# Attention plus two MLP blocks on one core: where the scores of the last 64 queries are computed, and in which PSUM tile

## Chip, cores and metric

One Trainium2 chip, one of its cores. The time is the device time of one execution in microseconds (us): 447.11 us is the median of three executions of the kernel before (447.08 to 447.6). Engines are called by the names of the profile: PE is the matrix engine (PEld its weight loads), DVE the vector engine, ACT the scalar engine, POOL the GpSimd engine, SP the engine that issues the DMAs.

## What is computed

```python
def _attn_ref(q, k, v):                      # 2 batches, 12 heads, 448 tokens, 64 columns per head
    scores = scale * np.matmul(q, k.transpose(0, 1, 3, 2))
    scores = np.where(mask, -1000000000.0, scores)          # causal: keys behind the query
    scores = scores - np.max(scores, axis=-1, keepdims=True)
    attn = np.exp(scores)
    attn = attn / (np.sum(attn, axis=-1, keepdims=True) + 1e-09)
    return np.matmul(attn, v).astype(np.float32)
...
x = attn_out, heads side by side             # 896 tokens x 768
x = silu(x @ w_in) @ w_out                   # 768 -> 2048 -> 768
x = solu_layernorm(x @ w_in2) @ w_out2       # 768 -> 1024 -> 768
```

All data are fp32. The change lies in the attention alone, at the scores.

## The kernel before, in words

**Stages.** The attention takes about the first 80 us; then come the four matrix products (fp32 split into a high and a low part, three products each), which keep PE filled to the end.

**The attention loop.** The loop of line 342 has one iteration per head pair (two heads j = 0, 1 of one batch), 12 pairs in all, plus four iterations in which only late steps are left. Each engine works through its instructions in the order in which the program writes them, so the order of the statements in the loop is a schedule written out by hand. An iteration i does for pair i the scores, their maxima and exponentials; for pair i - 1 the reciprocals of the sums and the normalisation (`recip`, `norm`); for pair i - 2 the transposes of the normalised weights (`transp`) and their copies out of PSUM (`evict`); for pair i - 3 the product with v (`pv`); for pair i - 4 the split of that product's result into a high part (`pv_hi`, line 192, ACT) and a low part (`pv_lo`, line 197, DVE).

**Scores.** The queries of a head are cut into three blocks of 128 (c = 0, 1, 2) and a rest of 64 (c = 3). Because of the causal mask block c needs 128 (c + 1) key columns: 128, 256, 384, and 448 for the rest. For c = 0, 1, 2 there is a matrix product for each of the two heads, on one half of PE's rows each (line 117). For c = 3 both heads' 64 queries stand side by side in one zero-padded stationary operand of 128 rows (`q3s`), so that one product serves both heads; its 448 columns are cut into two halves of 224, one in each bank (line 109). Each fp32 product runs on PE as two passes, so the profile counts twice as many matmuls as the code writes.

**PSUM tiles of the scores.** The pool `pss` has two tiles of two banks each, `sa` and `sb`, one buffer each (bank j is head j). Before, `sa` holds the 384-column scores and, behind them in the same banks, the 128-column scores; `sb` holds the 256-column scores and behind them the two 224-column halves. A tile is written anew for the next pair only when all its readers are done. The readers are the maxima (`maxes`, line 128): one DVE instruction per block and head adds the mask, writes the result to SBUF and keeps the row's extremum. Their order on DVE is that of `UNITS`: the two 384-column blocks, the reciprocals of the pair before (lines 138, 139), `pv_lo`, the two 128-column blocks, the two 256-column blocks, the 448-column block, then the copies `evict` of groups 2 and 3 (line 173), one normalisation (line 146), and, from iteration 8 on, a piece of weight conversion (`feed`, lines 217 to 225) ahead of the next pair's maxima. In iteration 1 the order differs: four normalisations of pair 0 stand on DVE behind the maxima of pair 1.

**PSUM tiles of the transposes.** The pool `psx` has four one-bank buffers that go round. An iteration takes six: the transposes' groups 0 to 4 and the tile of `pv`. So group 3 gets the buffer in which the `pv` of the iteration before stands, and must wait until `pv_lo` has read it; group 4 gets the buffer of group 0, which ACT copies out in the same iteration. Groups 0 to 3 hold 3, 3, 4 and 2 transposes, group 4 holds 4.

PE's order in an iteration is thus: scores c = 2, 0, 1, 3; transposes groups 0, 1, 2, 3, 4; `pv`. After the last live iteration the space of `pss` goes to the first matrix product (`g1drain`, line 298).

Of the kernel before, what the change touches and what calls it, by code (L numbers as in the profile page):

```python
# [8 lines left out]
F32 = mybir.dt.float32  # L9
# [6 lines left out]
B, H, S, D = 2, 12, 448, 64  # L16
# [26 lines left out]
def fused(ctx, tc, qT, kT, vv, vt, w1, w2, w3, w4, gl, out):  # L43
    nc = tc.nc
    PS = bass.MemoryType.PSUM

    def pool(name, bufs=1, **kw):
        return tc.alloc_tile_pool(name=name, bufs=bufs, **kw)
# [12 lines left out]
    with tc.manual_schedule():  # L61
        att = pool("att", 2)
        psx = pool("psx", 4, space=PS)
        pss = pool("pss", 1, space=PS, side="right")
# [3 lines left out]
        QB, EB = 4, 3  # L68
        q3s = [att.tile([128, 2, C], F32, name=f"qt{n}", tag=f"qt{n}", bufs=1) for n in range(QB)]
# [28 lines left out]
        st, scs = {}, {}  # L98

        def scores(p, c):  # L100
            k, q, _ = raws[p]
            if c == 2:
                scs[p, "a"] = pss.tile([128, 2, 512], F32, name="sa", tag="sa")
            elif c == 1:
                scs[p, "b"] = pss.tile([128, 2, 512], F32, name="sb", tag="sb")
            elif c == 3:
                t = scs[p, 0, 3] = scs[p, "b"][:, :, 256:256 + S // 2]
                for j in range(2):
                    nc.tensor.matmul(t[:, j], q3s[p % QB], k[:, S // 2 * j:S // 2 * (j + 1)],
                                     start=True, stop=True)  # L110
                return
            t = scs[p, "b" if c == 1 else "a"]
            lo = 384 if c == 0 else 0
            for j in range(2):
                dst = scs[p, j, c] = t[:, j, lo:lo + wide(c)]
                r = slice(64 * j, 64 * j + 64)
                nc.tensor.matmul(dst, q[r, 128 * c:128 * c + 128], k[r, :wide(c)], start=True, stop=True)

        def ep(p, u):
            return es[p % EB][:, AT[u]:AT[u] + 4].rearrange("q b k -> q (b k)")[:, :wide(u[1])]  # L120

        def maxes(p, u):
            if p not in st:
                st[p] = att.tile([128, 4, 7], F32, name="st", tag="st", bufs=4)
            o, m = ep(p, u), (mask3 if u[1] == 3 else mask)[:, S - wide(u[1]):]
            if u[1] == 3:
                o, m = (a.rearrange("q (z k) -> q z k", z=2) for a in (o, m))
            nc.vector.tensor_tensor_reduce(  # L128
                o, scs[p, u[0], u[1]], m, -SCALE, 3.0e38,
                ALU.add, ALU.min, st[p][:, 0, COL[u]:COL[u] + 1])  # L130

        def exps(p, u):
            n = COL[u]
            nc.scalar.activation(ep(p, u), ep(p, u), AF.Exp, bias=st[p][:, 0, n:n + 1], scale=-1.0,  # L134
                                 accum_out=st[p][:, 1, n:n + 1])

        def recip(p):
            nc.vector.tensor_scalar(st[p][:, 2], st[p][:, 1], 1e-9, None, ALU.add)
            nc.vector.reciprocal(st[p][:, 3], st[p][:, 2])

        def norm(p, u, eng):
            r = st[p][:, 3, COL[u]:COL[u] + 1]
            if eng is nc.gpsimd:
                eng.tensor_tensor(ep(p, u), ep(p, u), r.to_broadcast([128, wide(u[1])]), ALU.mult)  # L144
            else:
                eng.tensor_scalar(ep(p, u), ep(p, u), r, None, ALU.mult)
# [7 lines left out]
        def transp(p, g):  # L154
            t = psx.tile([128, 4, 128], F32, name="tr", tag="x")
            for n, (j, c, kb) in enumerate(GROUPS[g]):
                nc.tensor.transpose(t[:, n], es[p % EB][:, AT[j, c] + kb], ident)  # L157
            trs[p, g] = t

        def evict(p, g):  # L160
            if g == 0:
                aT[p] = att.tile([128, NKB, 2, S], F32, name="aT", tag="aT")
            t, a = trs.pop((p, g)), aT[p]
            if g < 2:
                src, dst = t[:, :QC].rearrange("k c q -> k (c q)"), a[:, 0, g, :QC * 128]
            elif g < 4:
                w = 128 * (4 - g)
                src = t.rearrange("k c q -> k (c q)")[:, :2 * w].rearrange("k (j q) -> k j q", j=2)
                dst = a[:, g - 1, :, QC * 128 - w:QC * 128]
            else:  # L170
                src, dst = t.rearrange("k b (j q) -> k b j q", j=2), a[:, :, :, QC * 128:]
            if g in (2, 3):
                nc.vector.tensor_copy(dst, src)
            else:
                nc.scalar.activation(dst, src, AF.Copy)
# [14 lines left out]
        def pv_hi(p):  # L190
            b, hp = divmod(p, NP)
            nc.scalar.activation(xh[:, hp, b * S:b * S + S], pvs[p][:, :S], AF.Copy)
# [74 lines left out]
        def feed():  # L267
            m = fed[0]
            fed[0] += 1
            at = lambda a: order[a] if a < len(order) else None  # L270
            if m + 1 < len(order):
                conv_a(*order[m + 1])
            for _ in range(2):
                if len(pend) >= lag[0]:
                    finish(pend.pop(0))
            if m < len(order):
                n, c = order[m]
                conv_b(n, c, x3 if n == 3 else xs, at(m + 1))
                pend.append(m)
            if m + RAWS < len(order):  # L280
                load_w(*order[m + RAWS])
# [60 lines left out]
        for i in range(NP2 + TL + 2):  # L342
            live = i < NP2
            n, r, p, x = i - 1, i - TL, i - TL - 1, i - TL - 2
            doN, doT, doP, doX = (0 <= a < NP2 for a in (n, r, p, x))
            if doX:
                pv_hi(x)
            if doN:
                exps(n, UNITS[6])
            if live:  # L350
                for _ in range(FEEDS.count(i)):
                    feed()
                for c in (2, 0, 1, 3):
                    scores(i, c)
                for u in UNITS[:2]:
                    maxes(i, u)
                for u in UNITS[:2]:
                    exps(i, u)
            if i == 1:
                for u in UNITS[2:4]:  # L360
                    maxes(i, u)
            late = ()
            if doN:
                recip(n)
                dve = [u for u in KEYS if u[1] < 2] if n == 0 else KEYS if n == NP2 - 1 else KEYS[-1:]
                for u in KEYS:
                    if u not in dve:
                        norm(n, u, nc.gpsimd)
                if n == NP2 - 1:
                    for u in dve:  # L370
                        norm(n, u, nc.vector)
                else:
                    late = dve
            if doX:
                pv_lo(x)
            if live and i != 1:
                for u in UNITS[2:4]:
                    maxes(i, u)
            if doT:
                for g in range(4):  # L380
                    transp(r, g)
                evict(r, 0)
                transp(r, 4)
                evict(r, 1)
            if live:
                for u in UNITS[2:4]:
                    exps(i, u)
                for u in UNITS[4:6]:
                    maxes(i, u)
            if doT:  # L390
                evict(r, 4)
            if doP:
                for z in range(NKB):
                    pv(p, z)
            if live:
                for u in UNITS[4:6]:
                    exps(i, u)
                maxes(i, UNITS[6])
            if doT:
                for g in (2, 3):  # L400
                    evict(r, g)
            for u in late:
                norm(n, u, nc.vector)
            if not live:
                for _ in range(FEEDS.count(i)):
                    feed()
            if live and i + 3 < NP2:
                load_pair(i + 3)
                load_v(i + 3)
            if i == 1:  # L410
                for a in range(RAWS):
                    load_w(*order[a])
            if i == FEEDS[0] - 1:
                conv_a(*order[0])
                shift_w(*order[0])
            if i == NP2 - 1:
                pss.release()
                gm = pool("gm", 2, space=PS, side="right")
            for g in range(4):
                if GD[g] == i - NP2 + 1:  # L420
                    g1drain(g)
# [13 lines left out]
        for f in range(KF):  # L435
            if f == 1:
                gps[f, 1] = gm.tile([128, 512], F32, name="ps", tag="gm")
            else:
                t = pair()
# [3 lines left out]
            for half in range(2):  # L443
# [3 lines left out]
                m = 2 * f + half + 4  # L447
# [195 lines left out]
        for t in range(NT):  # L643
# [3 lines left out]
            z = t - NT + 2  # L647
# [61 lines left out]
```

## Time and profile before

| | |
|---|---|
| median of three executions | 447.11 us |
| the profiled execution | 447.77 us |
| its span in the profile | 446.0 us |
| PE busy | 437.3 us (98%) |
| DVE busy | 321.3 us (72%) |
| ACT busy | 224.2 us (50%) |
| POOL busy | 169.5 us (38%) |
| granted PE clock | 0.9 or more of full speed in each of 40 slices |

The profiled execution is 1.8 us longer than its span: the span runs from the program's first instruction to its last. A row of the timeline gives the start of a run of like instructions in us from the span's start, the time from there to the end of the last of them, engine, line and operation, output from input by tile name, the shape, how many, and in square brackets for how long the engine stood idle before it and who ended that. A matmul's end is modelled and lies behind the start of the next, since matmuls are pipelined.

### The profile page before, as it was taken

The numbers are of one execution on the slowest core, as the hardware profiler recorded it, in microseconds if no ns is written. First come the engines' busy times: TensorE is split into PE (matmuls) and PEld (weight loads), VectorE is DVE, ScalarE is ACT, GpSimd is POOL, SyncE is SP. The second block draws the span as 40 slices with busy tenths as digits, with TensorE's granted clock in tenths as the row PEclk, the third lists the DMA queues.
The fourth block names the chain that finished last, engine by engine and source line by source line (L and its number), as shares of the span: only waits on it lengthen the run. The fifth ranks groups of instructions, "written<-read, shape, count | busy, mean of one in ns | idle before, by whom it ended". The sixth has DMA issues, their size and how long they took to land.

```text
span 446.0 us, 6961 instructions
## 1 busy us (share of the span) xinstructions
PE 437.3 (98%) x2379; PEld 382.0 (86%) x2379; DVE 321.3 (72%) x705; ACT 224.2 (50%) x519; POOL 169.5 (38%) x189
## 2 busy tenths in 40 slices
PE   8899999999999999999999999999999999999997
PEld 5666666789999999999999999999888888999996
DVE  4978999669999998988775978756878787511110
ACT  4988998444434434344443434433647765712121
POOL 2745656336777666665423324332500000000000
PEclk9999999999999999999999999999999999999999
DMA  5776311205533424242745557564023220010101
GB/s 162 203 252 184 113 47 37 72 0 143 141 102 112 136 77 141 79 135 77 233 142 186 180 144 217 172 209 119 23 71 106 80 63 1 35 37 35 55 35 54
DMA packets 26387, 49.22 MB, mean 110 GB/s; under 512 B 6128, under 2 KB 13936, under 8 KB 26352
## 3 DMA queue, kind: packets, MB, share of 16 engines
q1 hardware_dynamic: 26352, 48.77, 36.6%
q8 instruction: 19, 0.31, 0.3%
q14 instruction: 16, 0.13, 0.1%
HBM read 46.01 MB, written 2.75 MB: 109 GB/s over the span
## 4 chain that ended last, share of the span: by engine, by line
PE 89%; DVE 7%; ACT 3%; issue 0%; DVEq 0%; ACTq 0%
PE h L298 8%; PE h L299 8%; PE h L300 8%; PE h L465 7%; PE h L464 7%; PE h L463 7%; PE ps L631 4%; PE ps L632 4%; PE ps L633 4%; PE h L576 4%; PE h L578 4%; PE h L577 4%; PE pv L186 4%; DVE e L128 3%; PE tr L157 2%; ACT e L134 2%
## 5 line engine op out<-in xcount | busy, mean ns | idle before, releaser
L236 POOL TENSOR_TENSOR wl<-wx,wh 128x384 fp32r<-128x384 f32 x64 | 77.8, 1218 | 98.1 <-ACT wh L235 93.0
L210 ACT ACTIVATE wr<-wr 128x384 f32<-128x384 f32 x96 | 52.7, 554 | 34.0 <-DMA wr<-w_in 33.8
L235 ACT ACTIVATE wh<-wx 128x384 fp32r<-128x384 f32 x64 | 33.4, 522 | 67.8 <-DVE wx L220 30.8
L220 DVE SCALAR_TENSOR_TENSOR wx<-wr,wx 128x384 uint32<-128x384 uint32 x96 | 66.4, 692 | 0.0
L300 PE MATMUL h<-xh,wl 128*128 128x448 f32 x174 | 63.5, 365 | 0.0
L299 PE MATMUL h<-xl,wh 128*128 128x448 f32 x174 | 63.5, 365 | 0.0
L298 PE MATMUL h<-xh,wh 128*128 128x448 f32 x174 | 63.5, 365 | 0.0
L225 DVE TENSOR_SCALAR wr<-wr 128x384 uint32<-128x384 uint32 x96 | 58.5, 609 | 5.0 <-DMA wr<-w_in 4.7
L217 DVE SCALAR_TENSOR_TENSOR wx<-wr 128x384 uint32<-128x384 uint32 x96 | 58.3, 607 | 1.4 <-POOL gl L308 1.3
L465 PE MATMUL h<-gh,wl 128*128 128x448 f32 x160 | 58.3, 364 | 0.0
L463 PE MATMUL h<-gh,wh 128*128 128x448 f32 x160 | 58.2, 364 | 0.0
L464 PE MATMUL h<-gl,wh 128*128 128x448 f32 x160 | 58.2, 364 | 0.0
L308 POOL TENSOR_TENSOR gl<-sg,gh 128x448 fp32r<-128x448 f32 x32 | 41.1, 1286 | 21.5 <-DVE gh L307 10.7
L134 ACT ACTIVATE e<-e,st 128x384 f32<-128x384 f32 (+3 forms) x84 | 43.7, 523 | 9.3 <-DVE st L128 9.1
L144 POOL TENSOR_TENSOR e<-e,st 128x384 f32<-128x384 f32 (+3 forms) x63 | 37.5, 630 | 28.4 <-PE tr L157 17.4
L631 PE MATMUL ps<-w4h,lh 128*128 128x384 f32 (+2 forms) x112 | 38.3, 342 | 0.0
L632 PE MATMUL ps<-w4l,lh 128*128 128x384 f32 (+2 forms) x112 | 37.8, 337 | 0.0
L633 PE MATMUL ps<-w4h,ll 128*128 128x384 f32 (+2 forms) x112 | 37.8, 337 | 0.0
L620 DVE TENSOR_TENSOR ll<-tp,lh 128x512 fp32r<-128x512 f32 x14 | 9.0, 685 | 37.9 <-ACT lh L619 37.9
L299 PEld LDWEIGHTS h<-xl,wh 128*128 128x128 f32 x174 | 32.7, 188 | 2.6
L298 PEld LDWEIGHTS h<-xh,wh 128*128 128x128 f32 x174 | 32.7, 188 | 2.6
L300 PEld LDWEIGHTS h<-xh,wl 128*128 128x128 f32 x174 | 32.7, 188 | 2.6
(99 smaller groups left out, 844.5 us busy)
## 6 DMA issues: line engine op xcount, KB each, us to landing
wr<-w_in SPq DMA_DIRECT2D x96, 384.0 KB, 3.6
k<-kT_in SPq DMA_DIRECT2D x12, 224.0 KB, 2.9
q<-qT_in SPq DMA_DIRECT2D x12, 192.0 KB, 3.1
v<-vv_in SPq DMA_DIRECT2D x12, 192.0 KB, 2.9
out<-o SPq DMA_DIRECT2D x12, 192.0 KB, 1.9
qt<-qT_in SPq DMA_DIRECT2D x24, 16.0 KB, 2.7
v<-vt_in SPq DMA_DIRECT2D x12, 32.0 KB, 2.5
out<-o SPq DMA_DIRECT2D x1, 256.0 KB, 2.0
```

What stands on the lines that cost most here:

```text
L217: nc.vector.scalar_tensor_tensor(xu, high, 0x80000000, low, ALU.bitwise_and, ALU.bitwise_or)
L220: nc.vector.scalar_tensor_tensor(xu, high, 3, xu, ALU.logical_shift_left, ALU.bitwise_or)
L225: nc.vector.tensor_scalar(low, low, 29, None, ALU.logical_shift_right)
L236: (lo_engine or nc.gpsimd).tensor_tensor(l, x, h.bitcast(F32), ALU.subtract)
L298: nc.tensor.matmul(ps[:, :S], wh, rh, start=k == 0, stop=False)
L299: nc.tensor.matmul(ps[:, :S], wh, rl, start=False, stop=False)
L300: nc.tensor.matmul(ps[:, :S], wl, rh, start=False, stop=k == KD - 1)
L463: nc.tensor.matmul(ps[:, :S], wh, rh, start=f == 0, stop=False)
L464: nc.tensor.matmul(ps[:, :S], wh, rl, start=False, stop=False)
L465: nc.tensor.matmul(ps[:, :S], wl, rh, start=False, stop=f == KF - 1)
L631: nc.tensor.matmul(ps[:, :w], lh[:, k], w4h[:, k, ns], start=k == 0, stop=False)
L632: nc.tensor.matmul(ps[:, :w], lh[:, k], w4l[:, k, ns], start=False, stop=False)
```

## The change

The 128-column scores move from tile `sa` to tile `sb`, behind the 256-column scores (columns 256 to 383); the order of the first three becomes 2, 1, 0. The scores of the last 64 queries become one matmul of 448 columns (one bank) instead of two of 224. They get a new `sa` tile, which has to wait for the maxima of the same pair's 384-column scores, and they are issued behind the transposes' groups 0 to 3 and ahead of group 4 (in the first two iterations, which have no transposes, behind the other scores). The maximum over them reads 448 columns in one piece instead of two times 224. Nothing else changes: no DMA, no DVE, ACT or POOL instruction is added, taken away or put elsewhere in its queue.

```diff
             elif c == 3:
-                t = scs[p, 0, 3] = scs[p, "b"][:, :, 256:256 + S // 2]
-                for j in range(2):
-                    nc.tensor.matmul(t[:, j], q3s[p % QB], k[:, S // 2 * j:S // 2 * (j + 1)],
-                                     start=True, stop=True)
+                t = pss.tile([128, 2, 512], F32, name="sa", tag="sa")
+                t = scs[p, 0, 3] = t[:, 0, :S]
+                nc.tensor.matmul(t, q3s[p % QB], k, start=True, stop=True)
                 return
-            t = scs[p, "b" if c == 1 else "a"]
-            lo = 384 if c == 0 else 0
+            t = scs[p, "a" if c == 2 else "b"]
+            lo = 256 if c == 0 else 0
...
             o, m = ep(p, u), (mask3 if u[1] == 3 else mask)[:, S - wide(u[1]):]
-            if u[1] == 3:
-                o, m = (a.rearrange("q (z k) -> q z k", z=2) for a in (o, m))
...
-                for c in (2, 0, 1, 3):
+                for c in (2, 1, 0):
                     scores(i, c)
                 for u in UNITS[:2]:
                     maxes(i, u)
                 for u in UNITS[:2]:
                     exps(i, u)
+            if i < 2:
+                scores(i, 3)
...
             if doT:
                 for g in range(4):
                     transp(r, g)
+                if live:
+                    scores(i, 3)
                 evict(r, 0)
                 transp(r, 4)
```

## Rows read from the trace of the kernel before

**Rows 1.** The page: engine busy time, and the granted PE clock by slice.

```profile
PE 437.3 (98%) x2379; PEld 382.0 (86%) x2379; DVE 321.3 (72%) x705; ACT 224.2 (50%) x519; POOL 169.5 (38%) x189
...
PEclk9999999999999999999999999999999999999999
```

**Rows 2.** Busy time by engine over the stretch behind the attention, 82 to 446 us.

```profile
82.00:446.00 364.00, 360.81 (x1843) 329.53 (x1839) 253.05 (x448) 156.19 (x300) 126.64 (x107) 1.00 0.35 105
```

**Rows 3.** Timeline of PE, iteration 5; the first row is of the stretch 30.7 to 31.0 alone.

```profile
30.34 0.92 PE L117 MATMUL sa<-k,q 64*128 64x384 f32 x4
...
30.34 1.14 PE L117 MATMUL sa<-k,q 64*128 64x384 f32 x8
...
31.84 1.02 PE L109 MATMUL sb<-k,qt 128*128 128x224 f32 x4
32.70 1.93 PE L157 MATMUL tr<-ident,e 128*128 128x128 f32 x16
```

**Rows 4.** Timeline of DVE, iteration 5.

```profile
31.63 0.56 DVE L128 CUSTOM_DVE_ANT_0 e<-sa,mask 128x384 f32<-128x384 f32 x1 [1.09 <-PE sa L117]
...
32.91 0.57 DVE L197 TENSOR_TENSOR xl<-pv,xh 128x448 fp32r<-128x448 f32 x1
...
34.51 0.62 DVE L128 CUSTOM_DVE_ANT_0 e<-sb,mask 128x448 f32<-128x448 f32 x1
```

**Rows 5.** Timeline of DVE: the first maximum of pairs 4, 7, 8, 9, 10, 11.

```profile
25.32 0.56 DVE L128 CUSTOM_DVE_ANT_0 e<-sa,mask 128x384 f32<-128x384 f32 x1 [2.02 <-PE sa L117]
...
44.12 0.56 DVE L128 CUSTOM_DVE_ANT_0 e<-sa,mask 128x384 f32<-128x384 f32 x1 [1.01 <-PE sa L117]
...
50.94 0.56 DVE L128 CUSTOM_DVE_ANT_0 e<-sa,mask 128x384 f32<-128x384 f32 x1
...
57.19 0.56 DVE L128 CUSTOM_DVE_ANT_0 e<-sa,mask 128x384 f32<-128x384 f32 x1 [1.01 <-PE sa L117]
...
63.55 0.55 DVE L128 CUSTOM_DVE_ANT_0 e<-sa,mask 128x384 f32<-128x384 f32 x1
...
70.57 0.55 DVE L128 CUSTOM_DVE_ANT_0 e<-sa,mask 128x384 f32<-128x384 f32 x1
```

**Rows 6.** Timelines: DVE in iteration 8; PE in 8, 10, 11, groups 3 and 4.

```profile
52.23 0.57 DVE L197 TENSOR_TENSOR xl<-pv,xh 128x448 fp32r<-128x448 f32 x1
...
52.95 0.99 PE L157 MATMUL tr<-ident,e 128*128 128x128 f32 x6 [0.26 <-DVE xl L197]
...
66.28 0.84 PE L157 MATMUL tr<-ident,e 128*128 128x128 f32 x6 [0.52 <-DVE xl L197]
...
73.22 0.85 PE L157 MATMUL tr<-ident,e 128*128 128x128 f32 x6 [0.52 <-DVE xl L197]
...
76.03 0.47 PE L298 MATMUL ps<-xh,wh 128*128 128x448 f32 x1
```

**Rows 7.** Timelines of DVE, PE and ACT, iterations 0 to 3.

```profile
6.80 0.55 DVE L128 CUSTOM_DVE_ANT_0 e<-sa,mask 128x384 f32<-128x384 f32 x1
...
8.39 0.62 DVE L128 CUSTOM_DVE_ANT_0 e<-sb,mask 128x448 f32<-128x448 f32 x1
...
9.02 0.56 DVE L128 CUSTOM_DVE_ANT_0 e<-sa,mask 128x384 f32<-128x384 f32 x1
...
10.66 0.17 DVE L138 TENSOR_SCALAR st<-st 128x7 f32<-128x7 f32 x1 [0.17 <-ACT e L134]
...
9.16 0.70 PE L117 MATMUL sb<-k,q 64*128 64x256 f32 x4 [0.19 <-DVE st L128]
...
16.67 0.63 PE L157 MATMUL tr<-ident,e 128*128 128x128 f32 x4 [1.19 <-ACT aT L175]
...
21.41 0.66 PE L157 MATMUL tr<-ident,e 128*128 128x128 f32 x4 [0.35 <-ACT aT L175]
...
14.84 0.62 ACT L134 ACTIVATE e<-e,st 128x384 f32<-128x384 f32 x1 [0.61 <-DVE st L128]
```

**Rows 8.** One line's instructions: L109's weight loads in iteration 5 (ns, min/median/max).

```profile
L109 PEld LDWEIGHTS sb<-k,qt x4: 186/190/190, 31.8 to 32.3; 128*128 128x128 f32 x4
```

## Prediction

> **What bounds the kernel now.** I read the page first, then the busy time behind the attention, then the timelines of PE and DVE side by side through the attention, where the change lies. The page has PE busy 98% of the span [rows 1], and from 82 us on it stands idle for 3.2 of 364 us [rows 2]. So whatever moves the moment at which PE leaves the attention moves the end by as much, and the question is what sets that moment. The attention has three regimes.
>
> In iterations 4 to 7 PE sets the pace. DVE waits about 1 us for PE before each pair's first maximum [rows 4, 5], and the mean cycle from one such maximum to the next is (44.12 - 25.32) / 3 = 6.27 us [rows 5]. In iteration 5 that maximum starts at 31.63, 0.15 us behind the end (30.34 + 1.14 = 31.48) of all eight passes into tile `sa`, the 128-column scores among them, although the 384-column passes that it reads end at 30.34 + 0.92 = 31.26 [rows 3, 4].
>
> In iterations 8, 10 and 11 DVE has weight conversions on top. Its first maxima have no wait before them there [rows 5], and PE in turn stops 0.26, 0.52 and 0.52 us before its last six transposes, released by `xl` of line 197 [rows 6]. Six transposes are groups 3 (two) and 4 (four): group 3 needs the buffer that `pv_lo` frees. That wait is the one to watch.
>
> At the start DVE and ACT set the pace: ACT waits for DVE's maximum at 14.84, and PE waits for ACT's copies at 16.67 and 21.41 [rows 7].
>
> **What the change does, step by step.** I write T for the start of a pair's 384-column scores on PE and D for the start of its first maximum.
>
> First maximum. `sa` then holds only the 384-column scores, so D comes 0.22 us earlier (31.48 - 31.26): T + 1.07 instead of T + 1.29 (31.63 - 30.34) [rows 3, 4]. A gain, where DVE waits for PE.
>
> The matmul itself. Two halves of 224 take 32.70 - 31.84 = 0.86 us to the next instruction [rows 3]. One piece of 448 streams as many columns: two passes of 448 at 0.22 us for two passes of 128 make 0.75. I take 0.80, between the bounds 0.75 and 0.86. The maximum over it I leave at the 0.62 of the two halves: in one piece it can't be under the 0.56 of 384 columns nor over 0.56 x 448 / 384 = 0.65 [rows 4].
>
> The transposes move up by those 0.86 us, and this is where it goes wrong. Group 3 comes behind ten transposes, so before at 32.70 + 10 x 0.11 = 33.80, while `xl` ends at 32.91 + 0.57 = 33.48; PE starts 0.15 behind such an end (52.95 against 52.23 + 0.57 = 52.80) [rows 6], so 0.17 us was left [rows 3, 4]. Now group 3 comes at T + 2.69 at latest by the same count (33.80 - 0.86 = T + 2.60, and up to 0.1 for the change of the array's shape, which moves from the last-64 scores to the transposes). But `xl` ends at D + 1.85 (33.48 - 31.63) = T + 2.92, and PE goes on at T + 3.07 [rows 3, 4]. **PE stops for 0.4 us in every iteration, and the last-64 scores, which stood ahead of that wait, now stand behind it.** Behind them queue group 4, `pv` and the next pair's scores. From the restart to the end of `pv` the rows have 76.03 - 73.22 = 2.81 [rows 6]. The new cycle is 1.07 + 1.85 + 0.15 + 2.81 + 0.80 = **6.68 us**, against 6.27.
>
> The last maximum. The last-64 scores start about 0.25 behind the restart (two transposes and the restart's own gap), last 1.02 to their end [rows 3], and DVE follows 0.15 later: `xl`'s end + 0.15 + 0.25 + 1.0 + 0.15 = + 1.55. DVE is ready for them at 34.51 - 33.48 = + 1.03 [rows 4]. So DVE waits **0.5 us** (bounds 0.4 to 0.6), and behind it wait the copies of groups 2 and 3, a normalisation and the weight conversion. Where DVE idles later anyhow this costs nothing; that cover is gone where a weight conversion follows (pairs 8, 10, 11).
>
> The start. In iteration 0 the last-64 scores have to wait for the second maximum, which ended at 6.80 + 0.55 = 7.35, now 7.13; start 7.2, end 8.2, their maximum at 8.4 instead of 8.39 - 0.22, done at 9.0. Only then is `sa` free for pair 1, whose first maximum therefore comes at 9.1 + 1.07 = 10.2 instead of 9.02 [rows 7]; before, only the 256-column scores waited for this (PE at 9.16). Of the 1.2 us some 0.25 come back, because DVE waited for ACT before the reciprocals at 10.66. ACT's own wait of 0.61 at 14.84 shows that DVE is the late one, so **0.9 us** goes on through ACT's unbroken queue to PE's wait at 21.41 [rows 7]. Bounds: 0 if ACT had been the late one, which row 14.84 speaks against, and 1.2.
>
> The copies by ACT, POOL's normalisations and SP's loads keep their places; group 4's copy gets some 0.5 us later, which ACT's waits of 0.6 us before the first exponential absorb. I cost them at nothing.
>
> **The sum**, as the delay of D, whose old values are in [rows 5]:
> - pair 4: 0.9 - 0.22 = 0.68;
> - pairs 5, 6, 7: 6.68 for 6.27, so 3 x 0.41 = 1.23, together 1.91;
> - pair 8 (DVE's pace): + 0.5 = 2.41;
> - pair 9: old 57.19 - 50.94 = 6.25, new 6.68: + 0.43 = 2.84;
> - pairs 10 and 11 (DVE's pace): + 0.5 each = 3.84;
> - the last `pv`, behind the last-64 scores of pair 11: + 0.80 = **4.64**.
>
> The profiled execution (447.77, with 1.8 outside the span) would become 452.4. The median before is 0.66 below it, 447.1, and gives **451.7**. With 0.75 or 0.86 for the matmul, 0.4 or 0.6 for DVE's wait and 0.6 to 1.2 for the start it lies between 451 and 453.
>
> **Rivals.** A change under 0.2% (0.9 us) can't be told from none here.
>
> *Faster: PE stays the pace, and the shorter matmul is a plain gain.* It decides at group 3: if `xl` were free before PE comes there, PE would neither stop nor push anything behind it, and 0.11 us (0.86 to 0.75) would be saved in each of 12 iterations: 1.3, so 445.8. Against it stands that `xl` hangs on D by 1.85 us of DVE work and only 0.17 us was left; for it only that PE shows no such stop in iterations 4 to 7 now. The half of the weight loads that is saved would lie behind this case: four loads of 0.19 us [rows 8], but four load-and-stream pairs take 0.86 in all [rows 3], about what their 896 columns take to stream, so the loads are hidden. The Trainium skill, "TensorE: Matmul & The Clock Gate", section "Back-to-back issue gap", says that in a stream of weight loads and matmuls the spacing is set by both. By that rule, with loads in full, four pairs of 0.19 + 0.19 would become two of 0.19 + 0.375, 0.39 less per iteration and up to 4.7 in all, which would wipe out the forecast's delay. The trace does not bear that out here, by the 0.86. Chance 0.05.
>
> *No change: the start alone.* If group 3's wait is met by slack but the start costs 0.68: 447.8, within 0.2%. Chance 0.06.
>
> *The tile doesn't free the first maximum.* If the first maximum still waited for all three early products, D would be 0.75 us later (the 256- and the 128-column passes), cycles 7.4, and the delay would come to some 9.8: 457. The old trace speaks against it: the wait ended with the tile's own last pass, not with the next tile's. Chance 0.05.
>
> *The clock falls.* PE idles more between 6 and 14 us. At 1.2 instead of 2.4 GHz, pair 1's 384-column scores (1.07) and one restart-to-`pv` stretch (2.81) would take twice as long: 1 to 4 us more, 453 to 456. An idle of 1.19 at 16.67 left the granted clock at 0.9 or more [rows 1, 7], and I expect no longer one. Chance 0.04.
>
> *Forecast* 0.80. It carries the range: from 449.3 (the start and the waits of the last maximum both half hidden) to 453.3 (every bound high). Faster 0.05, same 0.06, slower 0.89.
>
> **What would show it.** Right: PE stops about 0.4 us or more before the two transposes of group 3 in iterations 4 to 11, released by `xl`; the last-64 scores come right behind these; DVE waits about 0.5 us for PE before each 448-column maximum; the first maximum starts 1.07 behind T; cycles of 6.7 in pairs 4 to 7; pair 1's first maximum at 10.2; gemm rows start near 80.6 instead of 76.03. Wrong: no stop at group 3, or the first maxima of pairs 8, 10, 11 at their old distances, or pair 1 starting near 9.

## The result, and the profile after

The changed kernel takes 451.14 us (median of six executions, 450.79 to 454.71) against 447.5 of the kernel before in the same runs: ratio 1.0087, 95% interval 1.0066 to 1.0107. It is slower, by 3.9 us on the ratio and 3.6 by the medians; 4.6 was forecast.

A few executions of either kernel take some 3 us longer than the rest, and the profiled one is such: 454.71 us with a span of 452.9, where the other spans are 449.0 to 449.5. From the first row of the first matrix product to the end it has 452.9 - 79.58 = 373.3 us, the kernel before 446.0 - 76.03 = 370.0 [rows 6], with the same instructions. The extra 3.3 lie in the matrix products, where matmuls took a little longer each, as one of the page's groups shows (after first, then before; behind the bar the busy time in us and the mean in ns). The other five spans leave no room for them, so they are not put down to the change, and what follows reads the attention alone.

```profile
L295 PE MATMUL h<-xh,wh 128*128 128x448 f32 x174 | 64.0, 368 | 0.0
```

```profile
L298 PE MATMUL h<-xh,wh 128*128 128x448 f32 x174 | 63.5, 365 | 0.0
```

PE leaves the attention at 79.58 instead of 76.03, 3.55 later. The timeline of PE in iteration 5 of the changed kernel, which answers to [rows 3]:

```profile
31.40 0.92 PE L116 MATMUL sa<-k,q 64*128 64x384 f32 x4
32.15 0.82 PE L116 MATMUL sb<-k,q 64*128 64x256 f32 x8
32.90 1.31 PE L154 MATMUL tr<-ident,e 128*128 128x128 f32 x10
34.48 0.41 PE L154 MATMUL tr<-ident,e 128*128 128x128 f32 x2 [0.26 <-DVE xl L194]
34.72 0.92 PE L109 MATMUL sa<-k,qt 128*128 128x448 f32 x2
35.48 0.60 PE L154 MATMUL tr<-ident,e 128*128 128x128 f32 x4
36.01 2.10 PE L183 MATMUL pv<-aT,v 128*64 128x448 f32 x16
...
79.58 0.47 PE L295 MATMUL ps<-xh,wh 128*128 128x448 f32 x1
```

Ten transposes, then a stop that `xl` ends, then the two of group 3, then the last-64 scores, then group 4 and `pv`: the order of the forecast. The bracket's 0.26 us counts from the modelled end of the tenth transpose. By starts, the eleventh should come 0.11 behind the tenth (33.94) and comes 0.54 behind it, so the stop costs 0.43. From the scores at 31.40 to those of the next pair at 38.03 it is 6.63 us.

DVE's side, in the same iteration, answers to [rows 4]:

```profile
32.48 0.56 DVE L125 CUSTOM_DVE_ANT_0 e<-sa,mask 128x384 f32<-128x384 f32 x1 [1.41 <-PE sa L116]
...
33.76 0.57 DVE L194 TENSOR_TENSOR xl<-pv,xh 128x448 fp32r<-128x448 f32 x1
...
35.68 0.62 DVE L125 CUSTOM_DVE_ANT_0 e<-sa,mask 128x448 f32<-128x448 f32 x1 [0.24 <-PE sa L109]
...
37.16 0.54 DVE L143 TENSOR_SCALAR e<-e,st 128x448 f32<-128x448 f32 x1
```

The first maximum comes 32.48 - 31.40 = 1.08 behind the scores (1.29 before). `xl` ends at 34.33, and PE goes on 0.15 later. The 448-column maximum waits 0.24 us for its scores. And the normalisation behind it took 0.54 us, where 0.87 stood before: that row was not in the forecast, and it matters below.

The first maxima of pairs 4 and 7 to 11, which answer to [rows 5]:

```profile
25.84 0.56 DVE L125 CUSTOM_DVE_ANT_0 e<-sa,mask 128x384 f32<-128x384 f32 x1 [1.80 <-PE sa L116]
...
45.74 0.56 DVE L125 CUSTOM_DVE_ANT_0 e<-sa,mask 128x384 f32<-128x384 f32 x1 [1.41 <-PE sa L116]
...
52.66 0.55 DVE L125 CUSTOM_DVE_ANT_0 e<-sa,mask 128x384 f32<-128x384 f32 x1
...
59.66 0.56 DVE L125 CUSTOM_DVE_ANT_0 e<-sa,mask 128x384 f32<-128x384 f32 x1 [1.77 <-PE sa L116]
...
66.32 0.56 DVE L125 CUSTOM_DVE_ANT_0 e<-sa,mask 128x384 f32<-128x384 f32 x1 [0.23 <-PE sa L116]
...
73.28 0.55 DVE L125 CUSTOM_DVE_ANT_0 e<-sa,mask 128x384 f32<-128x384 f32 x1
```

Their delay against the kernel before, step by step beside the forecast's sum:

| | before | after | delay | forecast |
|---|---|---|---|---|
| pair 4 | 25.32 | 25.84 | 0.52 | 0.68 |
| pair 7 | 44.12 | 45.74 | 1.62 | 1.91 |
| pair 8 | 50.94 | 52.66 | 1.72 | 2.41 |
| pair 9 | 57.19 | 59.66 | 2.47 | 2.84 |
| pair 10 | 63.55 | 66.32 | 2.77 | 3.34 |
| pair 11 | 70.57 | 73.28 | 2.71 | 3.84 |
| PE leaves | 76.03 | 79.58 | 3.55 | 4.64 |

The start, in the timelines of PE and DVE, answers to [rows 7]: pair 1's scores wait 0.83 us for a maximum of pair 0 and its own first maximum comes at 10.03 instead of 9.02.

```profile
6.12 0.56 DVE L125 CUSTOM_DVE_ANT_0 e<-sa,mask 128x384 f32<-128x384 f32 x1 [4.65 <-PE sa L116]
...
9.07 0.59 PE L116 MATMUL sa<-k,q 64*128 64x384 f32 x2 [0.83 <-DVE st L125]
...
10.03 0.56 DVE L125 CUSTOM_DVE_ANT_0 e<-sa,mask 128x384 f32<-128x384 f32 x1 [1.02 <-PE sa L116]
...
24.77 0.92 PE L116 MATMUL sa<-k,q 64*128 64x384 f32 x4
```

The same rows of the kernel before:

```profile
6.31 0.56 DVE L128 CUSTOM_DVE_ANT_0 e<-sa,mask 128x384 f32<-128x384 f32 x1 [4.84 <-PE sa L117]
...
24.03 1.14 PE L117 MATMUL sa<-k,q 64*128 64x384 f32 x8
```

Pair 0's first maximum, which the change does not touch, begins 0.19 earlier in the changed kernel's profile. Counted from there, pair 1's first maximum comes 1.20 us later (3.91 for 2.71), PE's start of pair 4 0.93 (18.65 for 17.72), and every delay of the table is 0.19 larger: 0.71 at pair 4, 3.74 at the end.

### The profile page after: what moved, and what is told of

Its sections match the earlier page's. It is cut to its first block, busy times and chain, and to the rows that moved or that the text cites. A ratio compares the mean times of both kernels' runs of the same rounds, so it can differ in the third digit from the quotient of the medians.

```text
span 452.9 us, 6912 instructions
## 1 busy us (share of the span) xinstructions
PE 441.3 (97%) x2355; PEld 379.2 (84%) x2355; DVE 321.0 (71%) x705; ACT 225.0 (50%) x519; POOL 168.0 (37%) x189
## 4 chain that ended last, share of the span: by engine, by line
PE 89%; DVE 7%; ACT 2%; issue 1%; DVEq 0%; ACTq 0%
PE h L297 8%; PE h L295 8%; PE h L296 8%; PE h L465 7%; PE h L464 7%; PE h L466 7%; PE pv L183 4%; PE ps L632 4%; PE ps L634 4%; PE ps L633 4%; PE h L579 4%; PE h L577 4%; PE h L578 4%; DVE e L125 3%; PE tr L154 2%; PE sa L116 2%
## 5 line engine op out<-in xcount | busy, mean ns | idle before, releaser
L233 POOL TENSOR_TENSOR wl<-wx,wh 128x384 fp32r<-128x384 f32 x64 | 76.4, 1196 | 103.7 <-ACT wh L232 99.4
L222 DVE TENSOR_SCALAR wr<-wr 128x384 uint32<-128x384 uint32 x96 | 60.4, 630 | 2.7 <-DMA wr<-w_in 2.2
```

Of the source, the lines that this page charges most:

```text
L222: nc.vector.tensor_scalar(low, low, 29, None, ALU.logical_shift_right)
L233: (lo_engine or nc.gpsimd).tensor_tensor(l, x, h.bitcast(F32), ALU.subtract)
```

## The experiments

Four things were open: whether the wait for `pv_lo` with the scores behind it is what makes the cycle long; what the start costs by itself; what place and tiles do alone; and why the pairs that DVE paces lost less than forecast. "PE leaves" below is the first row of the first matrix product in each profile. Profiles differ by up to 1.0 us in when pair 0's first maximum begins (5.53 to 6.55), so distances within a profile are the firmer reading.

**Three groups instead of four.**

```diff
-                for g in range(4):
+                for g in range(3):
                     transp(r, g)
                 if live:
                     scores(i, 3)
+                transp(r, 3)
```

> The changed kernel, but the last-64 scores stand behind groups 0 to 2 and ahead of group 3. My theory (the wait of group 3 for pv_lo, with the last-64 scores queued behind it, makes the loop long): PE now reaches group 3 about 0.8 us later, at T + 3.5, behind the T + 3.07 at which its buffer is free, so there is no stop in iterations 4 to 7 and their cycle falls from 6.63 to about 6.2 us; the 448-column maxima find their scores ready. The start still costs what it costs in the changed kernel (+0.5 for pair 4's first maximum). In all 447.2 to 447.9, no different from before. Rival 1 (it is the new tile's waits, not the place, that cost): no change against the changed kernel, 451. Rival 2 (the start alone costs): 451 as well.

Measured: 448.2 us (the kernel before 447.96 in the same runs), ratio 1.0006 (0.9998 to 1.0015); the time is 0.3 us above the expected range, the ratio is that of no change. The timeline of PE, iteration 5:

```profile
32.48 1.31 PE L154 MATMUL tr<-ident,e 128*128 128x128 f32 x10
33.63 0.92 PE L109 MATMUL sa<-k,qt 128*128 128x448 f32 x2
34.38 0.82 PE L154 MATMUL tr<-ident,e 128*128 128x128 f32 x6
35.13 2.10 PE L183 MATMUL pv<-aT,v 128*64 128x448 f32 x16
```

No bracket is left: the scores fill the time in which `pv_lo` runs, and the cycle of pairs 4 to 7 is 6.18 us. Moving one matmul ahead of two transposes brings the ratio from 1.0087 to 1.0006. Both rivals fall.

**The low part first.** The changed kernel, with `pv_lo` ahead of the maxima:

```diff
-            if doX:
+            if doX and not live:
                 pv_lo(x)
...
+                if doX:
+                    pv_lo(x)
                 for u in UNITS[:2]:
                     maxes(i, u)
```

> The changed kernel, but on DVE pv_lo stands ahead of the pair's first maximum instead of behind the second and the reciprocals. My theory: pv_lo then ends by T + 1.3, group 3 finds its buffer free, PE never stops there in iterations 4 to 7, their cycle is 6.2; the first maximum comes 0.2 later in T, which PE's pairs don't feel. In the pairs that DVE paces the 0.5 us of pv_lo stand in the way of the first maximum: some 0.5 lost in each of pairs 8 and 10. In all 447.3 to 448.5. Rival (the last-64 scores' own waits, not pv_lo, hold PE): PE stops as before and 451 stays.

Measured: 448.48 us, ratio 1.0013 (1.0005 to 1.0022). PE runs twelve transposes in one go and leaves the last-64 scores where the change put them:

```profile
31.86 1.53 PE L154 MATMUL tr<-ident,e 128*128 128x128 f32 x12
33.23 0.92 PE L109 MATMUL sa<-k,qt 128*128 128x448 f32 x2
```

The cycle is 6.18 again. So the scores' place costs nothing in itself; it costs because `pv_lo` was late. The price named in the expectation shows too: the distance from pair 7's first maximum to pair 8's grows to 7.35 us from 6.82, that from pair 9's to pair 10's to 6.87 from 6.36.

**The old start.** The changed kernel, with the old tiles, order and halves for pairs 0 and 1 (here the part that counts):

```diff
-                for c in (2, 1, 0):
+                for c in (2, 0, 1) if i < 2 else (2, 1, 0):
                     scores(i, c)
...
-            t = scs[p, "a" if c == 2 else "b"]
-            lo = 256 if c == 0 else 0
+            t = scs[p, "a" if c == 2 or c == 0 and p < 2 else "b"]
+            lo = (384 if p < 2 else 256) if c == 0 else 0
```

> The changed kernel, but pairs 0 and 1 keep the old tiles, order and two halves. My theory of the start (pair 1's 384-column scores wait for pair 0's 448-column maximum): pair 1's first maximum is back at 9.0 from 10.0, the four normalisations begin at 12.2 instead of 12.9, PE starts pair 4 at 24.0 instead of 24.8, and 0.7 us of the loss are gone: 450.4. The cycles of pairs 4 to 7 stay at 6.6. Rival (the start's delay is absorbed later, by the pairs that DVE paces): 451.1, as the changed kernel.

Measured: 450.43 us, ratio 1.0057 (1.0045 to 1.0069). Pair 1's first maximum is back at 8.94, and the cycles of pairs 4 to 7 stay at 6.63. Pair 0's first maximum and PE's start of pair 4:

```profile
6.24 0.56 DVE L133 CUSTOM_DVE_ANT_0 e<-sa,mask 128x384 f32<-128x384 f32 x1 [4.76 <-PE sa L122]
...
23.93 0.92 PE L122 MATMUL sa<-k,q 64*128 64x384 f32 x4
```

Between them lie 17.69 us, 18.65 in the changed kernel and 17.72 in the kernel before. The intervals of the two ratios still overlap by a hair (1.0066 to 1.0069), so it is the profiles that carry this point: the start costs 0.9 to 1.0 us. PE leaves 1.21 us earlier than in the changed kernel (78.37), because the step from pair 8 to pair 9 is shorter too, 6.63 for 7.00; more on that below.

**The order alone.** The kernel before, with both halves behind the four groups and nothing else:

```diff
-                for c in (2, 0, 1, 3):
+                for c in (2, 0, 1):
                     scores(i, c)
...
                     transp(r, g)
+                if live:
+                    scores(i, 3)
```

> The kernel before, all its tiles and halves kept; only the two halves of the last-64 scores move behind the transposes' groups 0 to 3. My theory: the place alone makes the loop of pv_lo, group 3, last-64 scores, group 4, pv and next scores the pace. Without the 0.22 us of the earlier first maximum the loop is 1.29 + 1.85 + 0.15 + 2.81 + 0.86 = 6.96 us in PE's pairs, worse than the 6.63 of the changed kernel, and PE stops about 0.6 us at group 3. No cost at the start. Together 451.5 to 452.5. Rival 1 (the new sa tile is what costs): 447.5. Rival 2 (place and tiles cost about half each): 449.5.

Measured: 453.51 us, ratio 1.0141 (1.0119 to 1.0163); that is above the expected range. PE stops at group 3 (0.64 us by starts) and the cycle of pairs 4 to 7 is 6.86, near the 6.96 expected. What I had not seen is in DVE's timeline:

```profile
35.92 0.42 DVE L128 CUSTOM_DVE_ANT_0 e<-sb,mask 128x256 f32<-128x256 f32 x1 [0.94 <-PE sb L109]
```

The 256-column maximum waits for the 224-column halves, which it doesn't read, because they stand in the same tile. So the last maximum comes 3.90 us behind the pair's first (2.88 before), and the pairs that DVE paces lose too (7.42, 6.94 and 7.71 us for 6.82, 6.36 and 7.02). The new tile of the change takes this wait away: its 256-column maxima wait for nothing.

**The tiles alone.** The changed kernel with the last-64 scores ahead of all transposes:

```diff
-                for c in (2, 1, 0):
+                for c in (2, 1, 0, 3):
                     scores(i, c)
...
-                if live:
-                    scores(i, 3)
                 evict(r, 0)
```

> The tiles and the one matmul of the changed kernel, but the last-64 scores stay ahead of the transposes. My theory: they then wait for their own pair's second maximum (D + 1.1), and all transposes stand behind them: the loop is 1.08 + 1.12 to their start, 0.76 for them, 1.74 for sixteen transposes, 2.05 for pv = about 6.8 us in pairs 4 to 7, no better than the 6.63 of the changed kernel; group 3 finds its buffer free. With the start's cost about + 3.5 in all, ratio 1.008. Rival (the tiles cost nothing but the start): + 0.5, ratio 1.001.

Measured: 453.59 us, ratio 1.0127 (1.0101 to 1.0152), more than the 1.008 expected. The scores wait for the second maximum of their own pair, as expected:

```profile
34.62 1.02 PE L109 MATMUL sa<-k,qt 128*128 128x448 f32 x2 [0.60 <-DVE st L125]
```

With everything behind them the cycle is 6.90 (6.8 expected). Pairs 8 and 10, which I had left unchanged, lose 0.51 and 0.54 us (7.33 and 6.90 for 6.82 and 6.36); pair 11 loses nothing (6.89 for 7.02). The start costs more as well: 20.91 us from pair 0's first maximum to pair 4's, 19.72 in the changed kernel. So each half of the change is worse alone than both together (PE leaves at 81.67 and 81.50, in the changed kernel at 79.58): the new tile needs a later place, and the later place needs its own tile. The place chosen was two transposes too late.

**A longer way for DVE.** The kernel before, with group 3's copy done twice:

```diff
             if g in (2, 3):
                 nc.vector.tensor_copy(dst, src)
+                if g == 3:
+                    nc.vector.tensor_copy(dst, src)
```

> The kernel before, with DVE's copy of group 3 done twice in each iteration (the second changes nothing in the data), so that DVE has 0.34 us more between the last maximum and its normalisation. It stands for the 0.3 us by which the changed kernel's last maximum comes later. My theory: the normalisation waits for POOL's last one anyway, so it starts 0.34 later, ends at the same time and is 0.34 shorter (0.53 instead of 0.87); the cycles of pairs 8, 10 and 11 stay at 6.8, 6.4 and 7.0: ratio 1.000 within 0.1%. Rival (my prediction's step: what stands behind that maximum is late by as much in the pairs that DVE paces): 0.34 more in three pairs, 1.0 us, ratio 1.0023.

Measured: 448.19 us, ratio 0.9997 (0.9978 to 1.0016). Three timelines, of DVE and POOL around one normalisation: the kernel before, the changed kernel, this one.

```profile
35.99 0.87 DVE L146 TENSOR_SCALAR e<-e,st 128x448 f32<-128x448 f32 x1
...
33.14 3.47 POOL L144 TENSOR_TENSOR e<-e,st 128x128 f32<-128x128 f32 x6 [2.84 <-PE tr L157]
```

```profile
33.98 3.47 POOL L141 TENSOR_TENSOR e<-e,st 128x128 f32<-128x128 f32 x6 [3.16 <-PE tr L154]
```

```profile
35.79 0.42 DVE L175 COPY aT<-tr 128x256 f32<-128x256 f32 x1
36.13 0.44 DVE L146 TENSOR_SCALAR e<-e,st 128x448 f32<-128x448 f32 x1
...
32.82 3.48 POOL L144 TENSOR_TENSOR e<-e,st 128x128 f32<-128x128 f32 x6 [2.83 <-PE tr L157]
```

POOL's six normalisations end at 36.61, 37.45 and 36.30; DVE's one ends at 36.86, 37.70 (from the row above) and 36.57: 0.25, 0.25 and 0.27 behind, whether it started early (0.87 long) or late (0.54, 0.44). With POOL quiet the same instruction takes 0.44 (in the order alone, from 38.09), so the hold of 0.87 can take in 0.43. Here the normalisation begins 0.45 us later in its pair (36.13 - 31.32 = 4.81 behind the first maximum, 35.99 - 31.63 = 4.36 before), which uses it up. The first maxima of pairs 8, 10 and 11 come 6.85, 6.38 and 7.09 us behind those of the pairs before them, for 6.82, 6.36 and 7.02 in the kernel before. So 0.34 us more work on DVE in each pair cost 0.12 in these three together, not 1.0.

**Both mends.** Three groups and the old start together (the two diffs above).

> Both mends at once: the last-64 scores behind groups 0 to 2 and ahead of group 3, and the old tiles and order for pairs 0 and 1. My theory (the place costs 3 us, the start 0.75, and the two add up): PE leaves the attention about 0.4 us earlier than before (first row of the first matrix product near 75.6 instead of 76.03), because PE's cycle is 6.18 instead of 6.25 in pairs 4 to 7 and the first maximum comes 0.2 earlier: ratio 0.999 to the kernel before, from 0.9975 to 1.0. Rival (what the start gives back is eaten by the pairs that DVE paces): 1.0006, as with three groups alone.

Measured: **446.95 us, ratio 0.9962 (0.9938 to 0.9986)**: faster than both kernels, and by more than the range expected; the rival's 1.0006 falls. By the medians (447.98 before) it is 1.0 us, a ratio of 0.9977, and eleven of the twelve executions lie below the lowest of the 29 of the kernel before. PE leaves the attention at 75.16, with cycles of 6.18 in pairs 4 to 7. Of the 0.87 us by which that is earlier, 0.26 come in pairs 5 to 7 and 0.24 in pair 9, as the expectation has it; 0.39 come in pair 11, which it did not have. There the reciprocals' first step in iteration 10 took 0.16 us for 0.91: it began at 64.03, just ahead of a POOL instruction at 64.05, and in the kernel before at 64.50, behind one at 64.38. What puts it ahead was not tried.

**The normalisation behind the weight conversion.** As before, and DVE's one normalisation is kept back until the next iteration's `feed` is done:

```diff
             for u in late:
-                norm(n, u, nc.vector)
+                if n == 0:
+                    norm(n, u, nc.vector)
+                else:
+                    held.append((n, u))
...
                 for _ in range(FEEDS.count(i)):
                     feed()
+                for m in held:
+                    norm(*m, nc.vector)
+                held.clear()
```

> As the one with both mends, and DVE's one normalisation of a pair moves behind the next iteration's weight conversion, away from POOL's normalisations. My theory: in the kernel before this instruction (0.87 us for 448 columns) ends 0.25 us behind POOL's last normalisation whatever its start, because it is held until POOL is through; away from POOL it takes 0.44, and the pairs that DVE paces get 0.2 to 0.4 us shorter each: 0.6 to 1.0 us less than with both mends alone, ratio about 0.9975 to the kernel before. Rival (0.87 is the price of 448 columns): no change from both mends alone, 0.999.

Measured: 447.54 us, ratio 0.9987 (0.9975 to 0.9998): no gain over both mends shows (446.95), so my expectation fell. The normalisation did drop to 0.44 or 0.45 us behind a conversion, but now the conversion's shift stands where it stood and is held in its place:

```profile
47.57 0.84 DVE L230 TENSOR_SCALAR wr<-wr 128x384 uint32<-128x384 uint32 x1
...
44.72 3.47 POOL L149 TENSOR_TENSOR e<-e,st 128x128 f32<-128x128 f32 x6 [2.71 <-PE tr L162]
```

POOL is through at 48.19, the shift at 48.41; the same shift takes 0.35 when POOL is quiet. So the wait comes with POOL's stretch: the next such instruction meets it. The rival I had set against it, that 0.87 is what 448 columns cost, falls as well.

## Why the forecast was right, and where its sum was not

**The loop through group 3: right, and shown.** The stop at group 3, the scores behind it and the cycle came as worked out (6.63 for 6.68; stop 0.43 for 0.4). The loop's terms are 1.08, 1.85 and 0.15 us, and 3.55 from the restart to the next pair's scores (38.03 - 34.48) for the forecast's 3.61. The stop goes when the scores stand ahead of group 3, and goes just as well when `pv_lo` comes earlier, with the scores left where the change put them.

**The first maximum and the matmul: right.** T + 1.08 for 1.07. The 448-column matmul takes 35.48 - 34.72 = 0.76 us; I had taken 0.80. (Two passes of 448 columns at 0.22 us for two of 128 make 0.77, not the forecast's 0.75.) The maximum over it still takes 0.62. It is the place and not the single piece that shortened it from 0.86: in the order alone the two halves, with four weight loads, stand in the same place and take 0.76 as well.

```profile
34.96 0.92 PE L109 MATMUL sb<-k,qt 128*128 128x224 f32 x4
35.72 0.60 PE L157 MATMUL tr<-ident,e 128*128 128x128 f32 x4
```

So the two weight loads that are saved are worth nothing that shows.

**The start: right.** Counted from pair 0's first maximum, pair 1's comes 1.20 us later for the 1.2 forecast, and PE's start of pair 4 0.93 for 0.9; with the old start both are gone (2.70 and 17.69 for 2.71 and 17.72).

**The term that failed is the last maximum's wait.** The forecast has "DVE waits 0.5 us ... that cover is gone where a weight conversion follows (pairs 8, 10, 11)" and puts 0.5 into the sum three times. Two things are off. The wait is 0.24 us and the maximum 3.20 - 2.88 = 0.32 later in its pair: the last-64 scores end 0.92 us behind their start, not 1.02, and DVE follows 0.04 behind that end (35.68 - 35.64), not 0.15. And the cover is not gone: behind the copies stands the normalisation, which in iterations 4 to 11 of both kernels ends 0.24 to 0.26 us behind POOL's last one. POOL's begin behind the reciprocals, 1.5 us behind the pair's first maximum in iteration 5 of both kernels (33.14 - 31.63 and 33.98 - 32.48), so a later last maximum shortens the hold and costs nothing, up to the 0.43 us between 0.87 and 0.44. Pairs 8, 10 and 11 lost 0.10, 0.30 and -0.06 us, 0.34 together, where the sum has 1.5. For pair 8 the row 0.54 for 0.87 returns 0.33, as much as the maximum was late; the 0.10 left is a wait of the weight conversion for ACT, which the kernel before does not have:

```profile
51.45 0.56 DVE L214 SCALAR_TENSOR_TENSOR wx<-wr 128x384 uint32<-128x384 uint32 x1 [0.21 <-ACT wr L207]
```

I had read the normalisation's 0.87 as the price of its 448 columns. The Trainium skill, "SBUF — State Buffer", section "Who interferes with whom", says that VectorE in a two-port mode and GpSimd contend for a shared pair of ports: whichever issues first has it for its whole instruction, and the other is blocked. The trace agrees that DVE is held while POOL runs, with 0.44 us unhindered and 0.87 held; that it is the ports is not shown by any run here. I had looked for such a hold only where an operation was added.

In pair 10 the gap is PE's new cycle (6.66 for 6.36). For pair 11 the hold moved: in iteration 10 the reciprocals' first step took 0.17 instead of 0.91, since it began at 67.28, ahead of the POOL instruction at 67.48; the normalisation took 1.15 instead of 0.80.

**What is left open.** From pair 8 to pair 9 the changed kernel needs 7.00 us, 0.3 more than the loop's 6.68. The chain shows 0.45 us before pair 9's first maximum in which DVE waits for nothing that the profile shows:

```profile
59.21 0.45 issue
```

The same pair starts its maximum 1.44 behind its scores in two other kernels, the one with three groups and the one with the tiles alone, but 1.07 or 1.08 in the three kernels with the old start. What it is was not tried.

**The sum.** In the profile it is 1.09 us too high (4.64 for 3.55): 1.16 at pairs 8, 10 and 11 and 0.13 in pairs 5 to 7, less 0.32 for pair 9 and 0.04 at the end, and 0.16 up to pair 4. The last is not the forecast's: 0.19 is the earlier begin of pair 0's first maximum. Without it the sum is 0.90 too high. That the time came out near is thus in part luck: pair 9's 0.32 us, which nobody forecast, stand against the 1.16.

**The rivals.** That PE stays the pace fell with the stop, that the start alone costs fell with the cycles, that the tile doesn't free the first maximum fell with T + 1.08. That the loads count in full fell with the 0.76 of four passes and of two. That the clock falls did not come about: the granted clock is 0.9 or more of full speed in each slice of the profile, the new idle stretches at the start among them, and 1.000 in the mean.

## What to carry to other kernels

When work moves behind other work in an engine's queue, its price is the wait that it lands behind. Find the instruction there that takes a buffer which another engine has to free, and put the work ahead of it. Where the buffers of a pool go round, the wait falls on one tile of the group (here group 3, two transposes), not on the whole group. And before a delay on a busy engine is put into the sum, look for the next instruction there that waits for somebody else anyway: it swallows delays up to its own slack.

## What was not expected of the hardware

A `TENSOR_SCALAR` of DVE, which reads and writes SBUF alone, shows no wait when it starts while POOL runs; it lasts longer. It ends shortly behind the end of a POOL instruction, whatever its start. 448 columns took 0.54 and 0.87 us that way and 0.44 with POOL quiet, and ended 0.24 to 0.26 behind; a shift of 384 columns took 0.84 and 0.35, and ended 0.22 behind; the reciprocals' first step, 7 columns, took 0.91 and 0.17, and ended 0.03 behind (before, 64.50 + 0.91 against 64.38 + 1.00). The hold can last over two POOL instructions. In the changed kernel's iteration 10 the normalisation began while POOL finished one instruction (to 71.12), and was held through the whole of the next:

```profile
71.01 1.15 DVE L143 TENSOR_SCALAR e<-e,st 128x448 f32<-128x448 f32 x1
...
71.08 0.82 POOL L141 TENSOR_TENSOR e<-e,st 128x384 f32<-128x384 f32 x1
```

But it need not last until POOL is through. In the kernel before, the normalisation of iteration 2 begins earlier in POOL's run and gets in between two instructions: it ends at 18.69, 0.26 us behind one of them (18.43), and POOL's last takes 0.97 us instead of the 0.83 of iteration 5.

```profile
18.07 0.62 DVE L146 TENSOR_SCALAR e<-e,st 128x448 f32<-128x448 f32 x1
...
17.82 0.61 POOL L144 TENSOR_TENSOR e<-e,st 128x256 f32<-128x256 f32 x1
...
18.39 0.97 POOL L144 TENSOR_TENSOR e<-e,st 128x384 f32<-128x384 f32 x1
```

The section of the Trainium skill named above ("SBUF — State Buffer", "Who interferes with whom") has the blocked engine wait for the other's one instruction; the trace agrees at 18.07, and shows two at 71.01.

A maximum that reads columns 0 to 255 of a tile waits for matmuls into columns behind them in the same tile (0.94 us in the order alone). Which matmuls share a tile decides what a reader waits for in these kernels; whether the chip or the program asks for that wait, no run here tells.
